# Split weight sums parked in HBM by the first pass and loaded by the second, and one more second-level product group, in a float32 FNet + GEGLU kernel

## The chip, the cores and the metric

One core of a Trainium2 chip runs the whole kernel. The metric is the device time of one execution in microseconds (us), as the median of several runs; less is better.

## The reference

The kernel computes, for x of 2048 rows and 512 columns,

```python
xn = layernorm(x)
a, b = xn @ dft_hid_re.T, xn @ dft_hid_im.T          # 512 x 512 matrices
y = dft_seq_re @ a - dft_seq_im @ b                  # 2048 x 2048 matrices
h = gelu_tanh(xn @ w_gate) * (xn @ w_up)             # 512 x 1792 each
out = x + y + h @ w_down                             # 1792 x 512
```

all in float32.

## The kernel before

Every float32 operand is split into a high and a low part, and each product of two tiles is three matmuls (high-high, low-high, high-low; `mm3`, L332). All large products go through one level of Winograd's form of Strassen's scheme: 2x2 blocks, seven products instead of eight. The products have the numbers 0 to 6 in the code. The operands that the scheme needs are sums of blocks, made on the vector engine (DVE), and split by the scalar engine (ACT, high part) and DVE (low part).

The program has a first half (layer norm, both DFTs; it fills about the first 380 us) and a second half in which the gate and up products are worked off in 28 *units* n = 0 to 27. There are 14 weight blocks (NP = 14) and two passes over them: units 0 to 13 use the first half of the rows of x, units 14 to 27 the second half, with the same weights. A product of a unit is two groups of three matmuls (six). Of the weights a unit loads two tiles `wx` (`load_w`), makes sums `ws` (`weight_sums`, L664), and splits tiles into `wh`/`wl` or, for halves, `w` (`weight_split`). In between stand the down products `dn` and what is left of the DFT (`y`).

For some of the products a second level is used (`inner`). Units n and n+1 (n even) and both passes together form a 2x2 of blocks for product r; seven *inner* products of three matmuls give what four plain products of six would give. `LEAD` says from which unit on this is done: product 0 and 4 from unit 0, product 1 from unit 4. The part of the result that belongs to the second pass is written to HBM (`m_park`, from POOL's queue) and read back by unit n + 14 (`load_m`, SP's queue, tiles `m0`), which then leaves that product out. Where products 0 and 4 are both taken over, the results enter the unit's accumulation in PSUM as a *seed* (an ACT copy).

In the second pass, units 24 to 27 read sums that the first pass had parked (`ws_park`); units 14 to 23 load the weights and make their sums again.

The order of the instructions on each engine is not that of the code: a planner (`Plan`) lists operations with costs, due times, buffer needs (109 slots of 256 KB, `SLOTS`) and limits on transfers in flight, and writes each engine's list from them. A buffer is given to a new tile as soon as the operations that use the old one are over, so an engine can have to wait for a DMA that still reads a buffer which it wants to write, and SP's queue for one that still reads the buffer that it wants to load into. Each engine works its own list in order. `add(name, engine, cost, fn, after, makes, uses, mb)` enters an operation; "p", "v", "a", "g", "s" are TensorE (PE), DVE, ACT, POOL (whose queue writes to HBM) and SP (whose queue reads from it).

Of the kernel before, what the change touches and what calls it, by code (L numbers as in the profile page):

```python
# [39 lines left out]
class Plan:  # L40
# [101 lines left out]
    def choose(self, ready, frees, spare):  # L142
        best = None
        for e, names in ready.items():
# [3 lines left out]
            for n, at in names.items():  # L148
# [134 lines left out]
def fnet_geglu_kernel(ctx: ExitStack, tc: tile.TileContext, x, xt, cs, dh, wgu, wd, out):  # L283
# [81 lines left out]
    m_park = dram.tile([3, NP, P, CH], F32, name="m_park")  # L365
    h_park = dram.tile([NP // 2, 4, P, CH], F32, name="h_park")
    x_park = dram.tile([2, 2, P, CH], F32, name="x_park")
    ws_park = dram.tile([2, NP, 2, P, D], F32, name="ws_park")
# [280 lines left out]
    wx, wl = {}, {}  # L649
# [23 lines left out]
    def trimmed(n, k):  # L673
        return isinstance(n, int) and k < 2 and lead(n - 1, 4 * k)

    def weight_split(n, k):
# [10 lines left out]
        for r, p in enumerate(((0, 1), (4, 5), (6, 2))[k]):  # L687
            wl[n, p] = v[0][:, r], v[1][:, r]
        if trimmed(n, k):
            v, src = ([t.rearrange("p a b -> p (a b)")[:, P:] for t in u] for u in (v, (wx[n][k],)))  # L690
# [10 lines left out]
    LEAD = {0: 0, 4: 0, 1: 4}  # L701
    M_PARK = {0: 0, 4: 1, 1: 2}
    KEEP_SUMS = (10, NP)
# [671 lines left out]
    def unit_at(n):  # L1375
        return TU + n * 17 * 3 * MM + min(max(n, 0), 4) * 2 * W
# [76 lines left out]
    def units():  # L1453

        def weights(m):
            name, at = m if isinstance(m, tuple) else (0, m)
            bare = fetched(m, 1)
            if short(m) or (bare and at >= NP + KEEP_SUMS[0]):
# [21 lines left out]
            for k in range(bool(bare), 3 if short(m) else 4):  # L1480
# [3 lines left out]
                         less=trimmed(m, k))  # L1484
        def park_sums(m, at, d):
# [98 lines left out]
        for r in LEAD:  # L1584
            for n in range(LEAD[r], NP, 2):
# [6 lines left out]
                for j in range(2):  # L1592
                    m = n + NP + j
                    add(("lm", m, r), "s", .45, lambda m=m, r=r: load_m(m, r), after=[("mp", m - NP, r)], mb=MB, makes={("m0", m, r): 1})
# [30 lines left out]
        def inner_p(n, r, k):  # L1625
# [10 lines left out]
            wait = {1: [("sb", n)] if r == 1 else [("ib", n, r)], 5: [("ib", n, r)], 6: [("iq", n, r)], 3: [("iw", n, r)], 2: [("iaw", n, r)]}  # L1636
# [15 lines left out]
        def park_m(n, m, r, to, ready):  # L1652
            add(("mp", m, r), "g", .6, lambda: nc.gpsimd.dma_start(m_park[M_PARK[r], m], side[n, to, r]), after=[ready], uses=[(to, n, r)], mb=MB)

        def plus_first(name, n, m, to):
            u = (n, to, 1)
            add((name, m), "v", V5, lambda: nc.vector.tensor_add(side[u], side[n, to, 0], side[u]),
                after=[("ia" + to[0], n, 1), ("ia" + to[0], n, 0)], uses=[(to, n, 1), (to, n, 0)])
# [320 lines left out]
```

## Time and profile before

| | |
|---|---|
| median of 3 runs | 782.89 us (782.74 to 783.1) |
| the profiled execution | 783.33 us, of which the span of the trace is 781.6 us |
| matmuls | 3432 |
| PE busy | 777.5 us, 99% of the span |
| DVE, ACT, POOL busy | 742.2 us (95%), 531.4 us (68%), 149.5 us (19%) |
| HBM | 131.33 MB read, 69.48 MB written, 257 GB/s over the span |
| granted TensorE clock | full in all 40 slices |

PE, DVE, ACT, POOL and SP are the engines; matmuls overlap, so that one lasts 389 ns in the records while the next starts sooner. "Idle before" in a group's row is the time that its engine stood still ahead of these instructions, and who ended it. A DMA has a time from its issue until its data has landed.

### The profile page before, as it was taken

Reading aid. Unit: us, or ns where it says so; the run is one execution under the profiler, and the core shown is the slowest. Engines: PE = TensorE matmul, PEld = TensorE weight load, DVE = VectorE, ACT = ScalarE, POOL = GpSimd, SP = SyncE. Lnnn points to the kernel's source line nnn. Section 1 sums busy time; section 2 is a strip of 40 time slices with the busy share of each in tenths; the row PEclk is TensorE's granted clock in tenths of the full one; section 3 lists DMA queues with packets and bytes.
Section 4 is the critical chain, followed back from the end, with each engine's and each line's share of the span. In section 5 each row is a group of like instructions: output and inputs, shape, how many; then the busy total and the mean of one; then the engine's idle time right before and its main releaser. Section 6 shows DMA issues by size and latency. Waiting matters only on the chain.

```text
span 781.6 us, 11754 instructions
## 1 busy us (share of the span) xinstructions
PE 777.5 (99%) x3432; PEld 642.2 (82%) x3432; DVE 742.2 (95%) x1410; ACT 531.4 (68%) x1006; POOL 149.5 (19%) x248
## 2 busy tenths in 40 slices
PE   9999999999999999999999999999999999999998
PEld 6888888888888888888888888888888888888887
DVE  7999999999899999999999998999999999997987
ACT  6998565566545374665776766867788887788841
POOL 0120420043221141000212221433100113220000
PEclk9999999999999999999999999999999999999999
DMA  9975997879999979993745544787996468996432
GB/s 329 386 200 164 382 339 245 272 259 274 348 385 387 338 280 377 392 326 118 176 151 160 187 144 156 282 288 273 382 394 238 104 144 161 258 266 215 147 123 108
DMA packets 100465, 198.48 MB, mean 254 GB/s; under 512 B 12176, under 2 KB 20912, under 8 KB 100208
## 3 DMA queue, kind: packets, MB, share of 16 engines
q1 hardware_dynamic: 77616, 134.01, 49.5%
q0 software_dynamic: 22496, 63.45, 27.3%
q8 instruction: 27, 0.44, 0.2%
q14 instruction: 38, 0.31, 0.1%
q10 hardware_dynamic: 288, 0.26, 0.1%
HBM read 131.33 MB, written 69.48 MB: 257 GB/s over the span
## 4 chain that ended last, share of the span: by engine, by line
PE 99%; DMA 0%; DVE 0%; ACT 0%; issue 0%
PE m L332 35%; PE b L332 22%; PE dn L332 17%; PE y L332 10%; PE c L332 8%; PE z L332 4%; PE a L332 3%; DMA x<-in_x 0%; DVE bn L400 0%; DVE p L1915 0%; DVE xa L423 0%; ACT w L411 0%; DVE stats L402 0%; PE st L1266 0%
## 5 line engine op out<-in xcount | busy, mean ns | idle before, releaser
L316 ACT ACTIVATE psh<-pan 128x512 fp32r<-128x512 f32 x203 | 118.2, 627 | 68.4 <-DVE pan L609 27.5
L321 DVE TENSOR_TENSOR psl<-pan,psh 128x512 fp32r<-128x512 f32 x198 | 128.6, 681 | 0.0
L332 PE MATMUL m<-psh,xch 128*128 128x512 f32 x232 | 90.2, 389 | 0.0
L332 PE MATMUL m<-psl,xch 128*128 128x512 f32 x232 | 90.2, 389 | 0.0
L332 PE MATMUL m<-psh,xcl 128*128 128x512 f32 x232 | 90.2, 389 | 0.0
L332 PEld LDWEIGHTS m<-psl,xch 128*128 128x128 f32 x232 | 43.6, 188 | 9.1
L332 PEld LDWEIGHTS m<-psh,xch 128*128 128x128 f32 x232 | 43.6, 188 | 9.1
L332 PEld LDWEIGHTS m<-psh,xcl 128*128 128x128 f32 x232 | 43.5, 188 | 8.9
L1645 ACT ACTIVATE w<-b 128x512 f32<-128x512 f32 x47 | 28.1, 598 | 29.8 <-PE b L332 28.9
L1736 POOL DMA_DIRECT2D partial<-part x28 | 24.5, 896 | 110.5 <-ACT part L1731 99.5
L609 DVE TENSOR_TENSOR pan<-pan 128x512 f32<-128x512 f32 x58 | 38.9, 680 | 3.2 <-DMA pan<-in_cs 3.2
L332 PE MATMUL m<-psh,xa 128*128 128x512 f32 x116 | 40.4, 389 | 0.0
L316 ACT ACTIVATE hth<-s 128x512 fp32r<-128x512 f32 x56 | 33.3, 627 | 10.4 <-DVE s L787 6.7
L1645 ACT ACTIVATE q<-b 128x512 f32<-128x512 f32 x47 | 28.1, 598 | 16.0 <-PE b L332 14.8
L321 DVE TENSOR_TENSOR wl<-ws,wh 128x512 fp32r<-128x512 f32 (+1 forms) x56 | 36.9, 668 | 1.5 <-ACT wh L316 1.3
L787 DVE TENSOR_TENSOR s<-s 128x512 f32<-128x512 f32 x56 | 36.2, 685 | 0.0
L321 DVE TENSOR_TENSOR htl<-s,hth 128x512 fp32r<-128x512 f32 x56 | 36.0, 686 | 0.1
L574 POOL DMA_DIRECT2D partial<-part x28 | 20.8, 790 | 79.0 <-ACT part L570 74.5
L1080 POOL DMA_DIRECT2D t_park<-pan x29 | 16.6, 573 | 98.6 <-DVE pan L610 91.2
L1649 DVE TENSOR_TENSOR w<-c,w 128x512 f32<-128x512 f32 x40 | 27.3, 689 | 6.8 <-ACT w L1645 6.5
L316 ACT ACTIVATE wh<-ws 128x512 fp32r<-128x512 f32 (+1 forms) x56 | 33.2, 609 | 0.0
L332 PE MATMUL dn<-hh,wh 128*128 128x512 f32 x84 | 32.7, 389 | 0.0
(790 smaller groups left out, 2431.9 us busy)
## 6 DMA issues: line engine op xcount, KB each, us to landing
pan<-in_cs SPq DMA_DIRECT2D x157, 256.0 KB, 6.4
partial<-part POOLq DMA_DIRECT2D x56, 256.0 KB, 6.4
wx<-in_wgu SPq DMA_DIRECT2D x48, 256.0 KB, 4.3
m<-m_park SPq DMA_DIRECT2D x38, 256.0 KB, 5.3
t_park<-pan POOLq DMA_DIRECT2D x29, 256.0 KB, 5.6
pan<-t_park SPq DMA_DIRECT2D x29, 256.0 KB, 5.9
h_park<-s POOLq DMA_DIRECT2D x28, 256.0 KB, 4.0
s<-h_park SPq DMA_DIRECT2D x28, 256.0 KB, 5.6
```

The costliest lines, as they stand in the source:

```text
L316: nc.scalar.activation(t[0], src, AF.Copy, scale=float(sign))
L321: engine.tensor_sub(t[1], src, hi)
L332: nc.tensor.matmul(ps, a[u][:, sl], b[v], start=first and r == 0, stop=last and r == 2, skip_group_check=resumed)
L574: nc.gpsimd.dma_start(partial[sp, r, j], ypart.pop((r, j)), **({} if r in (0, 5, 6) else {"accum_op": OP.add}))
L609: return [lambda: nc.vector.tensor_sub(t3, b22, b12), lambda: nc.vector.tensor_sub(t1, b12, b11), lambda: (nc.vector.tensor_sub(b22, *((t1 ...
L787: nc.vector.tensor_sub(t, u, v)
L1080: plan.add(("park", i), "g", .6, lambda: nc.gpsimd.dma_start(t2_park[c, k], pan_src[i][5]), after=[("S", i, 2)], mb=MB, uses=[("r", i, b22)])
L1645: nc.scalar.activation((bank if banks else side)[(n, to, *more)], src(), AF.Copy)
L1649: add((name, n, *more), "v", V5, lambda: nc.vector.tensor_add(side[(n, to, *more)], bank_of(n, c) if c == "c" else bank[(n, c, *more)], si ...
L1736: add(("da", *key), "g", .6, lambda: nc.gpsimd.dma_start(partial[sp, r, j], part[0], accum_op=OP.add), after=[("dc", *key), *sent], uses=[ ...
```

## The change

1. `LEAD[1]` goes from 4 to 2: units 2 and 3 (and with them 16 and 17) also form a second-level group for product 1.
2. The weights' split parts that the second pass needs (product 5, products 6 and 2, product 3; of units 2 to 13) are written to HBM from POOL's queue in the first pass (`park_w`, tensor `w_park`, 1 MB a unit, six DMAs), and units 16 to 27 load them ready to use (`load_half`, `load_whole`, four DMAs of 256 KB a unit). These units no longer load `wx`, make sums or split. Parking of sums (`ws_park`) for the gate and up weights is gone.
3. Additions of the inner products move from the first pass to the second: for product 4 the two summands are copied out by ACT and parked apart (`p2`, `r2`, `m_park` has a fourth part), and unit n + 14 adds them when it seeds its bank, on DVE instead of ACT. For product 1 the addition of the part of product 0 (`plus_first`) is gone, and the second pass adds (`iS`).
4. The planner counts a transfer as at least two when it looks whether a queue has room. The orders of DVE, ACT, SP and POOL change from there on in the first half too, in places; PE's stays the same there.

```diff
-                    k, room = self.parts(o), 8 if e == "s" else 7
+                    k, room = max(self.parts(o), 2), 8 if e == "s" else 7
...
-    LEAD = {0: 0, 4: 0, 1: 4}
-    M_PARK = {0: 0, 4: 1, 1: 2}
-    KEEP_SUMS = (10, NP)
+    LEAD = {0: 0, 4: 0, 1: 2}
+    M_PARK = {0: 0, 4: 1, 1: 2, "4": 3}
+    KEEP_SUMS = (NP, NP)
+    KEEP_SPLIT = 2
...
+            if not name and at >= NP + KEEP_SPLIT:
+                for k, (size, load) in enumerate(((1, load_half), (1, load_half), (2, load_whole), (1, load_half))):
+                    if k == 0 and bare:
+                        continue
+                    add(("lo", ("w", m, k)), "s", .45 * size, lambda k=k, load=load: load(m, k), after=[("pk", at - NP, k)],
+                        makes={("wl", m, k): size}, mb=size * MB, ahead=W_AHEAD)
+                return
...
+                if not name and KEEP_SPLIT <= at < NP and (k or not fetched(m + NP, 1)):
+                    add(("pk", m, k), "g", 1.2 if k < 3 else .6, lambda k=k: park_w(m, k), after=[("lo", ("w", m, k))], uses=[("wl", m, k)],
+                        mb=(1 + (k == 2)) * MB)
+
+        def park_w(m, k):
+            p = (1, 5, 6, 3)[k]
+            for h in range(2):
+                if k == 2:
+                    nc.gpsimd.dma_start(w_park[m, 1 + h], whole[m][h].bitcast(F32))
+                else:
+                    nc.gpsimd.dma_start(w_park[m, k // 3 * 3, :, h], wl[m, p][h].bitcast(F32))
+
+        def load_half(m, k):
+            t = slot("w", F32R, (P, 2, HD))
+            wl[m, (1, 5, 6, 3)[k]] = t[:, 0], t[:, 1]
+            nc.sync.dma_start(t.bitcast(F32), w_park[m - NP, (4, 0, 1, 3)[k]])
...
                     copy("iw", n, "w2", lambda: bank[n, "b2", r], [i], holds=[b2], more=(r,))
-                    sums("iaw", n, "w2", "c2", [("iw", n, r), ("i", n, r, 4)], c2, (r,))
-                    if r == 1:
-                        plus_first("iS", n, n + 1, "w2")
-                    park_m(n, n + 1, r, "w2", ("iS", n + 1) if r == 1 else ("iaw", n, r))
+                    if r != 4:
+                        sums("iaw", n, "w2", "c2", [("iw", n, r), ("i", n, r, 4)], c2, (r,))
+                    park_m(n, n + 1, r, "w2", ("iw" if r == 4 else "iaw", n, r))
+                elif k == 4 and r == 4:
+                    copy("ip", n, "p2", lambda: bank[n, "c2", r], [i], holds=[c2], more=(r,))
+                    park_m(n, n + 1, "4", "p2", ("ip", n, r))
+                elif k == 2 and r == 4:
+                    copy("ir", n, "r2", lambda: bank[n, "c2", r], [i], holds=[c2], more=(r,))
+                    park_m(n, n, "4", "r2", ("ir", n, r))
+                    park_m(n, n, r, "q2", ("iq", n, r))
...
-                nc.scalar.activation(bank[n, place], m0[n, r], AF.Copy)
+                if r == 4:
+                    nc.vector.tensor_add(bank[n, place], m0[n, r], m0[n, "4"])
+                else:
+                    nc.scalar.activation(bank[n, place], m0[n, r], AF.Copy)
...
                 if fetched(n, 1):
-                    hidden(n, (0, 0), [("lm", n, 1)], lambda n=n: m0[n, 1], [], [("m0", n, 1)])
+                    add(("iS", n), "v", V5, lambda n=n: nc.vector.tensor_add(m0[n, 1], m0[n, 0], m0[n, 1]), after=[("lm", n, 0), ("lm", n, 1)],
+                        uses=[("m0", n, 0), ("m0", n, 1)])
+                    hidden(n, (0, 0), [("iS", n)], lambda n=n: m0[n, 1], [], [("m0", n, 1)])
```

In the built programs the counts change as follows: PE 3432 matmuls before, 3429 now; DVE 59 instructions fewer, ACT 35 fewer, POOL 80 DMAs more, SP 36 DMAs more.

PE, product 1 of unit 2 (`a`, weights `wh_4765`/`wl`), in the program before; operands xT10 and xT11 are the two row blocks of the first pass:

```order
L332 MATMUL a_4823<-xT10h_4123,wh_4765 128x512
L332 MATMUL a_4823<-xT10l_4124,wh_4765 128x512
L332 MATMUL a_4823<-xT10h_4123,wl_4766 128x512
L332 MATMUL a_4823<-xT11h_4131,wh_4765 128x512
L332 MATMUL a_4823<-xT11l_4132,wh_4765 128x512
L332 MATMUL a_4823<-xT11h_4131,wl_4766 128x512
```

and in the changed program, the inner products 0 and 1 of the new group of units 2 and 3:

```order
L332 MATMUL b2_5094<-xT10h_4135,wh_4818 128x512 [waits Activation_49]
L332 MATMUL b2_5094<-xT10l_4136,wh_4818 128x512
L332 MATMUL b2_5094<-xT10h_4135,wl_4819 128x512
L332 MATMUL a_4911<-xT11h_4200,wh_4818 128x512
L332 MATMUL a_4911<-xT11l_4201,wh_4818 128x512
L332 MATMUL a_4911<-xT11h_4200,wl_4819 128x512
```

The six matmuls of unit 2 are still there, in two halves with banks of their own; five more inner products of three stand in place of 18 plain matmuls of units 3, 16 and 17.

POOL's queue near the end of the first pass (units 12 and 13), before; `h_park` writes hidden values, `w2`/`q2` are results of inner products, and the semaphores after "waits" are those of an earlier transfer of this queue (DMASW) and of the engine that made the data:

```order
L1653 DMA m_park_81<-w2_6257 128x512 [waits DMASW7_49,DVE_49]
L1653 DMA m_park_81<-q2_6223 128x512 [waits DMASW0_49,DVE_49]
L1753 DMA h_park_82<-s_6101 128x512 [waits DMASW1_49,DVE_49]
L1753 DMA h_park_82<-s_6163 128x512 [waits DMASW2_49,DVE_49]
L1753 DMA h_park_82<-s_6190 128x512 [waits DMASW3_49,DVE_49]
L1653 DMA m_park_81<-w2_6392 128x512 [waits DMASW4_49,DVE_49]
L1653 DMA m_park_81<-q2_6358 128x512 [waits DMASW5_49,DVE_49]
```

and now:

```order
L1692 DMA m_park_81<-r2_6363 128x512 [waits DMASW1_49,Activation_49]
L1795 DMA h_park_82<-s_6266 128x512 [waits DMASW2_49,DVE_49]
L1692 DMA m_park_81<-w2_6389 128x512 [waits DMASW3_49,DVE_49]
L1795 DMA h_park_82<-s_6261 128x512 [waits DMASW4_49,DVE_49]
L1506 DMA w_park_84<-wh_6397 128x512 [waits DMASW5_49,Activation_49]
L1506 DMA w_park_84<-wl_6398 128x512 [waits DMASW6_49,DVE_49]
L1692 DMA m_park_81<-q2_6354 128x512 [waits DMASW7_49,DVE_49]
```

The two `w_park` writes have come in ahead of `q2_6354`. That tile's buffer goes to ACT's copy `w_6533`, which stands among these rows of ACT in the changed program (it waits for DMASW7, the write of `q2_6354`):

```order
L316 ACTIVATE wh_6518<-ws_6365 128x512
L1684 ACTIVATE p2_6524<-c2_6494 128x512 [waits DVE_49,PE_49]
L1684 ACTIVATE w_6533<-b_6444 128x512 [waits DMASW7_49,PE_49]
L1684 ACTIVATE w2_6544<-b2_6419 128x512 [waits PE_49]
L1684 ACTIVATE q2_6553<-b2_6427 128x512 [waits DVE_49,PE_49]
```

PE's matmuls that go on in bank `b_6444` wait for that copy; they start 34 matmuls after the last one that goes into `q2_6354`. Of all chains in the changed program from a matmul over one write to HBM to a matmul it is the shortest; before, the shortest had 49.

SP's queue where the loads for the first units of the second pass stand (16 to 18), before; DMASW3 is the write of the last inner result `q2_6539`:

```order
L655 DMA wx_6681<-in_wgu 128x512 [waits DMAHW1_49,DMASW6_49,DMASW2_49]
L655 DMA wx_6682<-in_wgu 128x512 [waits DMAHW2_49,PE_49]
L1598 DMA m0_6698<-m_park_81 128x512 [waits DMAHW3_49,DVE_49]
L1598 DMA m0_6716<-m_park_81 128x512 [waits DMAHW4_49,DMASW3_49,PE_49]
L655 DMA wx_6741<-in_wgu 128x512 [waits DMAHW5_49,PE_49]
L655 DMA wx_6742<-in_wgu 128x512 [waits DMAHW6_49,PE_49]
```

and now; DMASW4 in the row of `m0_6836` is the write of the last inner result `q2_6688`, whose buffer `m0_6836` gets:

```order
L1637 DMA m0_6836<-m_park_81 128x512 [waits DMAHW0_49,DMASW4_49,PE_49]
L1637 DMA m0_6838<-m_park_81 128x512 [waits DMAHW1_49,DVE_49]
L1513 DMA w_6848<-w_park_84 128x512 [waits DMAHW2_49,Activation_49]
L1520 DMA wh_6851<-w_park_84 128x512 [waits DMAHW3_49,PE_49]
L1520 DMA wl_6852<-w_park_84 128x512 [waits DMAHW4_49,PE_49]
L1513 DMA w_6873<-w_park_84 128x512 [waits DMAHW5_49,DVE_49]
```

Behind the load that waits there are now split weights that PE itself reads (`w_6848` is product 3 of unit 16, its first matmul 73 matmuls after the last one that goes into `q2_6688`), where before there were raw weights.

More of the change, by code (lines that the diff above doesn't have):

```diff
@@ L364, in fnet_geglu_kernel @@
     z_park = dram.tile([NC // 2, 2, 2, 2, P, CH], F32, name="z_park")
-    m_park = dram.tile([3, NP, P, CH], F32, name="m_park")
+    m_park = dram.tile([4, NP, P, CH], F32, name="m_park")
     h_park = dram.tile([NP // 2, 4, P, CH], F32, name="h_park")
     x_park = dram.tile([2, 2, P, CH], F32, name="x_park")
+    w_park = dram.tile([NP, 5, P, 2, HD], F32, name="w_park")
     ws_park = dram.tile([2, NP, 2, P, D], F32, name="ws_park")
@@ L647, in park_xT @@
             nc.gpsimd.dma_start(xT_hl[k, i, h], xT[1, k, i][h].bitcast(F32))
-    wx, wl = {}, {}
+    wx, wl, whole = {}, {}, {}
     def load_w(n):
@@ L673, in trimmed @@
     def trimmed(n, k):
-        return isinstance(n, int) and k < 2 and lead(n - 1, 4 * k)
+        return isinstance(n, int) and k < 2 and lead(n - 1, 4 * k) and 1 + (k == 0 and lead(n - 1, 1))
     def weight_split(n, k):
@@ L688, in weight_split @@
             wl[n, p] = v[0][:, r], v[1][:, r]
+        whole[n] = v
         if trimmed(n, k):
-            v, src = ([t.rearrange("p a b -> p (a b)")[:, P:] for t in u] for u in (v, (wx[n][k],)))
+            if k == 0 and lead(n - 1, 1):
+                v, src = ([t[:, :, P:] for t in u] for u in (v, (wx[n][k],)))
+            else:
+                v, src = ([t.rearrange("p a b -> p (a b)")[:, P:] for t in u] for u in (v, (wx[n][k],)))
             return v, src[0]
@@ L1375, in unit_at @@
     def unit_at(n):
-        return TU + n * 17 * 3 * MM + min(max(n, 0), 4) * 2 * W
+        return TU + n * 17 * 3 * MM + min(max(n, 0), 2) * 4 * W
     for k in range(HS):
@@ L1484, in weights, with load_whole @@
                          less=trimmed(m, k))
+                if not name and KEEP_SPLIT <= at < NP and (k or not fetched(m + NP, 1)):
[12 more added lines that the diff above has]
+            nc.sync.dma_start(t.bitcast(F32), w_park[m - NP, (4, 0, 1, 3)[k]])
+        def load_whole(m, k):
+            v = slot("wh", F32R, (P, 2, HD)), slot("wl", F32R, (P, 2, HD))
+            for r, p in enumerate((6, 2)):
+                wl[m, p] = v[0][:, r], v[1][:, r]
+            for h in range(2):
+                nc.sync.dma_start(v[h].bitcast(F32), w_park[m - NP, 1 + h])
         def park_sums(m, at, d):
@@ L1593, in units @@
                     m = n + NP + j
+                    if r == 4:
+                        add(("lm", m, "4"), "s", .45, lambda m=m: load_m(m, "4"), after=[("mp", m - NP, "4")], mb=MB, makes={("m0", m, "4"): 1})
                     add(("lm", m, r), "s", .45, lambda m=m, r=r: load_m(m, r), after=[("mp", m - NP, r)], mb=MB, makes={("m0", m, r): 1})
@@ L1652, in park_m @@
         def park_m(n, m, r, to, ready):
[L1653 to L1658, printed above, removed]
+            add(("mp", m, r), "g", .6, lambda: nc.gpsimd.dma_start(m_park[M_PARK[r], m], side[n, to, int(r)]), after=[ready], uses=[(to, n, int(r))], mb=MB)
         def first_block(n, m, to, ready, held):
@@ L1699, in f @@
                 bank[n, place] = ps_tile(place)
-                nc.scalar.activation(bank[n, place], m0[n, r], AF.Copy)
-            add((name, n), "a", A5, f, after=[("p", n - 1, 5 if place == "b" and fetched(n, 1) else 6), ("lm", n, r)], banks=[key], holds=[key], uses=[("m0", n, r)])
-        until = 4
+                if r == 4:
+                    nc.vector.tensor_add(bank[n, place], m0[n, r], m0[n, "4"])
+                else:
+                    nc.scalar.activation(bank[n, place], m0[n, r], AF.Copy)
+            both = [r, "4"][:1 + (r == 4)]
+            add((name, n), "v" if r == 4 else "a", V5 if r == 4 else A5, f, after=[("p", n - 1, 5 if place == "b" and fetched(n, 1) else 6), *(("lm", n, u) for u in both)], banks=[key], holds=[key], uses=[("m0", n, u) for u in both])
+        until = 2
         todo = [("y", r, j, g) for r in (5, 3) for j in range(2) for g in range(2)]
```

6 lines of the change are left out of this document (2 added, 4 removed).

## The prediction

> **What bounds the kernel now.** I read the page's busy line and its chain first, then the list of PE's waits, then the chain in order of time, and last the second half in stretches.
>
> ```profile
> PE 777.5 (99%) x3432; PEld 642.2 (82%) x3432; DVE 742.2 (95%) x1410; ACT 531.4 (68%) x1006; POOL 149.5 (19%) x248
> PE 99%; DMA 0%; DVE 0%; ACT 0%; issue 0%
> ```
>
> PE is busy 99% of the span and is the whole chain that ends last. DVE is close behind at 95%, so the two have to be told apart by who waits for whom. The list of PE's waits has one row:
>
> ```profile
> PE warm L828 <- PEq L1972: 0.8, 1, 0.8
> ```
>
> That is 0.8 us, once, at the very start. After it no matmul waited for DVE, ACT or a DMA long enough to be listed. The chain in order of time says the same; its columns are start, length, engine and tile:
>
> ```profile
> 5.44 33.49 PE z L332 x144
> ...
> 97.56 76.16 PE m L332 x336
> ```
>
> ```profile
> 759.88 18.52 PE dn L332 x93
> 778.40 0.02 issue
> 778.43 0.42 DVE p L1915
> ```
>
> Here 336 matmuls take 76.16 us, which is 0.2267 us each, and PE goes on from 5.44 to 778.40 us without a piece of anything else. So PE's time is its number of matmuls times 0.2267 us, with some 8.6 us at both ends (5.44 us until the first real matmul, 3.2 us after the last), and nothing else has a price as long as PE does not have to wait. DVE's 95% is cover that is used up nearly, but not beyond.
>
> One rule speaks against reading it so. The Trainium skill, in "Perfetto Trace Analysis", section "Identifying the Most-Contended Engine", says that matmul busy time is a poor measure and that the share of weight loads is to be used; by that PE stands at 82% and DVE at 95% would be the most contended engine. The trace decides by the missing waits; what the rule would make of the time is the last rival below.
>
> **The matmuls.** The new group takes product 1 of units 2, 3, 16 and 17: four plain products of six matmuls, 24, become seven inner ones of three, 21. That is the only change in PE's count, 3432 to 3429: 3 x 0.2267 = 0.68 us less. It lies on the path from end to end, since PE is the path.
>
> **DVE and ACT.** What leaves DVE are mainly sums and low splits of weights in the second pass; what comes are 26 additions of parked summands there. The rows that price them (line, operands, count, busy, mean ns):
>
> ```profile
> L664 DVE TENSOR_TENSOR ws<-wx 128x256 f32<-128x256 f32 x45 | 18.8, 418 | 0.0
> L321 DVE TENSOR_TENSOR wl<-ws,wh 128x512 fp32r<-128x512 f32 (+1 forms) x55 | 36.2, 668 | 1.5 <-ACT wh L316 1.3
> L774 DVE TENSOR_TENSOR s<-s,m 128x512 f32<-128x512 f32 x5 | 3.4, 685 | 0.2 <-ACT s L769 0.2
> L1649 DVE TENSOR_TENSOR q<-c,q 128x512 f32<-128x512 f32 x40 | 27.4, 684 | 0.5 <-PE c L332 0.3
> ```
>
> ```profile
> L1645 ACT ACTIVATE w<-b 128x512 f32<-128x512 f32 x47 | 28.1, 598 | 29.8 <-PE b L332 28.9
> ```
>
> ```profile
> L332 PE MATMUL m<-psh,xch 128*128 128x512 f32 x232 | 90.2, 389 | 0.0
> ```
>
> 58 instructions of 256 columns x 0.418 = 24.2 us, 12 low splits x 0.668 = 8.0 us and 22 additions of the first pass x 0.685 = 15.1 us go, 47.3 us; 26 additions x 0.685 = 17.8 us and seven instructions for the new group, about 3 us, come. Net about 26 us off DVE (742 to 716 us), and 35 activations at up to 0.60 us, 21 us at most, off ACT, although ACT gets 14 more copies in the first pass. On PE's path all this is worth nothing: no wait of PE on DVE or ACT is there to be removed. It costs nothing either. PE's shortest round through ACT has 6 matmuls in between in both programs (7 x 0.2267 = 1.59 us, against 0.39 us of a matmul and 0.60 us of a copy), and DVE only gets more room.
>
> **The transfers.** This is where the change can cost something. POOL issues 80 DMAs more, nearly all in the first pass; SP 36 more, in the second. In bytes that is about 15 MB more to write and 10 MB more to read on 198 MB. What matters is how long data take to land. The stretches of the end of the first pass and the start of the second (PE, PEld, DVE, ACT, POOL busy; clock, DMA share, GB/s):
>
> ```profile
> 535.00:550.00 15.00, 15.00 (x68) 12.43 (x67) 14.32 (x29) 11.31 (x21) 4.24 (x8) 1.00 0.86 309
> 550.00:565.00 15.00, 15.00 (x67) 12.41 (x67) 14.22 (x31) 10.62 (x22) 2.91 (x6) 1.00 1.03 382
> 565.00:580.00 15.00, 15.00 (x68) 12.42 (x67) 14.02 (x30) 11.29 (x24) 1.98 (x4) 1.00 1.05 400
> 595.00:610.00 15.00, 15.00 (x68) 12.43 (x67) 14.49 (x34) 13.71 (x28) 0.00 (x0) 1.00 0.23 82
> ```
>
> The DMA engines are full from 550 us on (the slices up to 595 us are alike) and mostly idle from 595 us, so before they ran ahead of the need there; the clock is full and PE never stops. The landing times of the parked inner results, written by POOL (530 to 560 us), and of all transfers of that tensor (560 to 600 us):
>
> ```profile
> L1653 POOL DMA_DIRECT2D m_park<-q x4: 542/542/542, 534.9 to 559.9; - x4
> ...
> DMA to landing us min/median/max: 3.6/5.5/6.7
> ```
>
> ```profile
> L1598 SPq DMA_DIRECT2D m<-m_park x13: 319/327/411, 561.8 to 595.4; - x13
> ...
> DMA to landing us min/median/max: 4.5/5.5/8.3
> ```
>
> *First place*, unit 13, near 541 us (counted back from the end, 1054 matmuls of which 24 are half ones): a write of an inner result holds the buffer that ACT's copy needs, and PE needs the copy 34 matmuls after the one that made the result. Time there: 34 x 0.2267 = 7.7 us. It takes 0.39 (matmul) + 0.68 (DVE sum) + 0.60 (copy) = 1.7 us beside the write, so 6.0 us are left for issue and landing. An issue keeps POOL for 0.54 us, so that 80 more take 43 us of an engine that is busy 19% of the span; that alone holds up nothing. The landing row, counted from the issue, says 3.6 to 6.7 us: from 2.4 us to spare to 0.7 us late. Two `w_park` writes now go just ahead of it. I take the median, 5.5 us, and no wait, 0.7 us as the upper end.
>
> *Second place*, unit 16, near 566 us: SP's queue stands at the load of `m0_6836` until the write of the last inner result is through, and the split weights behind it are read by PE directly. From the last matmul of that result to the first that reads `w_6848` there are 73 matmuls, 16.5 us. Needed: 0.39 + 0.68, the write's landing, the issues of the two loads ahead, 2 x 0.33 = 0.7 us, and the load's own landing. At the medians 1.1 + 5.5 + 0.7 + 5.5 = 12.8 us, 3.7 us to spare; at the maxima 1.1 + 6.7 + 0.7 + 8.3 = 16.8 us, 0.3 us late. The same load feeds DVE, which is in order, and a sum behind it is needed by PE 79 matmuls later, 17.9 us: with 4 x 0.685 = 2.7 us for DVE's instructions 1.1 + 5.5 + 5.5 + 2.7 = 14.8 us at the medians, 18.8 us at the maxima, 0.9 us late (the late ends overlap, so 0.9 us holds for both). Such standing of SP's queue is nothing new (waits of SP's queue: total, times, longest):
>
> ```profile
> SPq L1598 <- DMA m_park<-w: 27.0, 5, 8.1
> SPq L1598 <- DMA m_park<-q: 13.3, 4, 6.3
> ```
>
> It stood up to 8.1 us and PE did not notice. The loads behind have more room: the fifth (`w_6873`) is read 91 matmuls after, 20.6 us.
>
> A rule bears on this stretch. The Trainium skill, "HBM Reference", "Specifications (TRN2)", gives about 358 GB/s as a core's share, and about 425 GB/s for a core that streams alone. The row of 400 GB/s fits the second. By the first, an estimate, loads would land 400/358 = 12% later, 6.2 us instead of 5.5 us, which the second place still bears.
>
> So the middle of both unknown costs is 0 us, and their upper ends add up to 0.7 + 0.9 = 1.6 us. Below nothing they cannot go: there is no listed wait to win back.
>
> **The first half** is reordered a little on DVE, ACT, SP and POOL (where single transfers now count as two), with PE's order unchanged. PE had no wait there, and the same dependences stay, so I cost it at nothing; what covers it is again PE's queue of work.
>
> **The sum.** 783.33 - 0.68 = 782.65 us against the profiled execution. That one was 0.44 us above the median of the runs (782.89 us), so against the median 782.89 - 0.68 = 782.21 us. With 1.6 us of waits it would be 783.8 us.
>
> **Rivals.** *The forecast*, fewer matmuls and at most 1.6 us of new waits: 782.2 us (to 783.8), a change of -0.09% to +0.12%. I take 0.2%, 1.57 us, as what a measurement of this kernel can tell from no change, so this whole case counts as the same. Chance 0.80.
>
> *Slower: both queues full at the hand-over.* With 8 transfers of SP and 7 of POOL in flight, 15 x 0.262 MB at 400 GB/s take 9.8 us. If the additional writes fill POOL's queue up to the end of the first pass, both hops of the second place take that long: 1.1 + 9.8 + 0.7 + 9.8 = 21.4 us against 16.5 us, 4.9 us late, and the time is 782.2 + 4.9 = 787.1 us. It decides from 2.25 us of waiting (1.57 + 0.68), which is when the two landings together pass 17.0 us. For it speaks that the DMA engines are full there already; against it that the largest landing seen is 8.3 us with SP's queue full, that POOL is over with its writes soon after, and the idle 595 to 610 us. Chance 0.16.
>
> *Faster: DVE was the bound in truth.* Then the 26 us that it loses would show, 782.9 - 26 = 757 us. Its 95% speak for it, the one row of PE's waits against. Chance 0.02. (The section of "Perfetto Trace Analysis" in the Trainium skill that is named above would have it so.) The same again, 0.02, for some gain of over 1.57 us at the start or the end, of which the rows show none.
>
> *The change does not do what it says*, that is PE's count is down by three but the group's own round trips cost those 0.68 us again: 782.9 us. It lies in the first case.
>
> **How the numbers follow.** 782.2 us is the time of the likeliest case. Of its 0.80 I put the low end at 781.9 us (the runs spread 0.36 us) and the high end at 784.0 us, 783.8 us with half that spread; what is left out is the slower case but for its mildest part, and the faster one. Faster 0.04, same 0.80, slower 0.16.
>
> **What would show it.** In the changed profile: 3429 matmuls at 0.2267 us, PE still 99% of the chain, DVE near 716 us, ACT near 510 to 515 us, POOL near 193 us, some 223 MB moved, and no row among PE's waits but the first. A wait of `b` on ACT `w` near 541 us would be the first place; a wait of `b` on a DMA `w<-w_park` or of `c` on DVE `w` near 569 us the second. The prediction is wrong if such rows add up to over 2.25 us, or if PE's first matmul or the tail after the last has moved.

## The result, and the profile after

The changed kernel takes 787.17 us (785.27 to 789.24, 6 runs); the kernel before took 782.83 us beside it. The ratio is 1.0059, with a 95% interval of 1.0041 to 1.0076: 4.3 us or 0.6% slower. The forecast was 782.2 us and no change that can be measured. The profiled execution took 787.01 us, its span is 785.2 us, 3.6 us more than before.

Busy times, what was moved and the chain that ended last, from the page of the changed kernel:

```profile
PE 778.4 (99%) x3429; PEld 641.2 (82%) x3429; DVE 720.6 (92%) x1351; ACT 518.3 (66%) x971; POOL 192.1 (24%) x328
DMA packets 110515, 223.66 MB, mean 285 GB/s; under 512 B 14033, under 2 KB 21745, under 8 KB 110257
PE 96%; DMA 2%; ACT 1%; DVE 1%; issue 0%; DVEq 0%; ACTq 0%
```

The counts are those forecast or near them: 3429 matmuls, DVE 720.6 us where 716 was forecast, ACT 518.3 us where it was 510 to 515, 223.66 MB where it was 223. But the chain is no longer PE alone: PE is 96% of it, and not 99%. The list of PE's waits (total, times, longest) has two rows that it did not have:

```profile
PE b L332 <- ACT q L1684: 2.3, 2, 1.6
PE warm L834 <- PEq L2016: 0.8, 1, 0.8
PE m L332 <- ACT m L1116: 0.2, 1, 0.2
```

The list shows only what is idle time; measured as the time from one matmul to the next beyond 0.2267 us, the stops after the first 9 us add up to 4.06 us, against 0.09 us before: 0.85 us near 333 to 335 us (first half), 1.02 us at 509 us, 0.18 us at 512 us and 1.85 us at 561.7 us. With the 0.09 us of before and the three matmuls taken off, 4.06 - 0.09 - 0.68 = 3.3 us of the 3.6 us are accounted for; most of the rest is the tail after the last matmul, 3.4 us instead of 3.2 us.

The chain in order of time (start, length, engine and line) shows how the longest stop came about:

```profile
548.51 1.12 PE b L332 x5
549.63 9.21 DMA m<-m_park
558.84 0.03 issue
...
558.97 0.70 DVE m L1862
...
559.69 0.04 ACT s L775
...
560.23 0.58 ACT p L1684
560.81 0.30 ACT w L316
561.11 0.50 ACT q L1684
561.61 0.04 issue
561.65 2.34 PE b L332 x9
```

A load of a parked inner result takes 9.21 us to land. DVE stands at L1862, the addition `iS` that was moved into the second pass, until it is there. Behind it ACT stands at L775, the gelu of the sum, and behind that, in ACT's queue, the copies `p` and `q` and a split `w`. PE needs `q` and stops. The same chain stands before 509 us, with a load of 7.16 us. Neither of the two places named in the prediction (541 us and 566 us) has a stop.

### The profile page after: what moved, and what is told of

Read it like the earlier page. It is cut to its first block, busy times and chain, and to the rows that moved or that the text cites. A ratio compares the mean times of both kernels' runs of the same rounds, so it can differ in the third digit from the quotient of the medians.

```text
span 785.2 us, 11961 instructions
## 1 busy us (share of the span) xinstructions
PE 778.4 (99%) x3429; PEld 641.2 (82%) x3429; DVE 720.6 (92%) x1351; ACT 518.3 (66%) x971; POOL 192.1 (24%) x328
## 2 busy tenths in 40 slices
DMA packets 110515, 223.66 MB, mean 285 GB/s; under 512 B 14033, under 2 KB 21745, under 8 KB 110257
## 4 chain that ended last, share of the span: by engine, by line
PE 96%; DMA 2%; ACT 1%; DVE 1%; issue 0%; DVEq 0%; ACTq 0%
PE m L332 35%; PE b L332 20%; PE dn L332 17%; PE y L332 10%; PE c L332 8%; PE z L332 4%; DMA m<-m_park 2%; PE a L332 2%; PE warm L834 1%; DVE m L1862 0%; ACT wh L316 0%; ACT q L1684 0%; DVE c L1119 0%; DVE wil L321 0%; ACT wih L316 0%
## 5 line engine op out<-in xcount | busy, mean ns | idle before, releaser
L321 DVE TENSOR_TENSOR psl<-pan,psh 128x512 fp32r<-128x512 f32 x198 | 128.3, 680 | 0.0
L332 PE MATMUL m<-psh,xch 128*128 128x512 f32 x232 | 90.4, 389 | 0.1
L332 PE MATMUL m<-psl,xch 128*128 128x512 f32 x232 | 90.3, 389 | 0.0
L332 PE MATMUL m<-psh,xcl 128*128 128x512 f32 x232 | 90.3, 389 | 0.0
L332 PEld LDWEIGHTS m<-psh,xch 128*128 128x128 f32 x232 | 43.5, 188 | 9.6 <-DVE m L1121 0.5
L332 PEld LDWEIGHTS m<-psh,xcl 128*128 128x128 f32 x232 | 43.6, 188 | 9.1
L332 PEld LDWEIGHTS m<-psl,xch 128*128 128x128 f32 x232 | 43.6, 188 | 8.9
L332 PE MATMUL m<-psh,xa 128*128 128x512 f32 x116 | 40.4, 389 | 0.0
L321 DVE TENSOR_TENSOR htl<-s,hth 128x512 fp32r<-128x512 f32 x56 | 35.8, 682 | 1.4 <-ACT hth L316 1.3
L321 DVE TENSOR_TENSOR hl<-s,hh 128x512 fp32r<-128x512 f32 x42 | 27.2, 684 | 8.0 <-ACT hh L316 7.9
L332 PE MATMUL dn<-hh,wh 128*128 128x512 f32 x84 | 32.7, 389 | 0.0
L332 PE MATMUL dn<-hh,wl 128*128 128x512 f32 x84 | 32.7, 389 | 0.0
L332 PE MATMUL dn<-hl,wh 128*128 128x512 f32 x84 | 32.7, 389 | 0.0
```

The lines of the kernel that those rows point to most:

```text
L321: engine.tensor_sub(t[1], src, hi)
L332: nc.tensor.matmul(ps, a[u][:, sl], b[v], start=first and r == 0, stop=last and r == 2, skip_group_check=resumed)
```

## The experiments

Four explanations were held against each other. *Queue*: the moved addition stands first in DVE's queue, and what is behind it is late. *Traffic*: the writes of split weights make transfers land later, whoever waits for them. *Order*: each new order of the planner meets stops of some size somewhere. And for the first half, the planner's line that counts a transfer as two. Each kernel was timed beside the kernel before, 782.76 to 782.81 us in all of these comparisons.

### Parts undone, with the planner ordering anew

Product 1's addition back in the first pass:

```diff
+                    if r == 1:
+                        plus_first("iS", n, n + 1, "w2")
...
-                    add(("iS", n), "v", V5, lambda n=n: nc.vector.tensor_add(m0[n, 1], m0[n, 0], m0[n, 1]), ...
-                    hidden(n, (0, 0), [("iS", n)], lambda n=n: m0[n, 1], [], [("m0", n, 1)])
+                    hidden(n, (0, 0), [("lm", n, 1)], lambda n=n: m0[n, 1], [], [("m0", n, 1)])
```

> The changed kernel, but the addition of product 0's part to product 1's part stands in the first pass again, and the second pass's gelu reads the parked sum as before. Queue theory (the moved addition stands first in DVE's queue until two loads have landed, ACT's gelu stands behind it, ACT's copies behind that, and PE behind the copies): the waits of PE in the second half, 3.1 us in the trace of the changed kernel, go or fall below 0.7 us; the 0.9 us in the first half near 333 us stays; 784 us (783.5 to 784.8). Traffic theory (the writes and loads of split weights make every landing longer, whoever waits for it): ACT's gelu waits for its load itself and PE waits as long; 786.5 to 787.5 us. Order theory (any new order of the planner meets waits of that size by chance): waits somewhere else, 784 to 788 us.

Measured: 783.50 us, ratio 1.0008 (1.0000 to 1.0017). No stop is left in the second half; 0.9 us near 333 us stay.

No split weights parked:

```diff
-    KEEP_SUMS = (NP, NP)
-    KEEP_SPLIT = 2
+    KEEP_SUMS = (10, NP)
+    KEEP_SPLIT = NP
```

> The changed kernel without the parking of split weights: no split weights are written or loaded, units 14 to 23 of the second pass load and split weights and units 24 to 27 read parked sums, as in the kernel before. The moved additions and the additional group stay. Traffic theory: landings of the parked inner results fall back to the 5.5 us median of before, no wait of PE in the second half, 783.1 us with the 0.9 us of the first half left (782.2 without). Queue theory: the addition still waits for two loads at the head of DVE's queue, so at least 1.5 of the 3.1 us stay: 784 to 787 us. Order theory: anything from 783 to 787 us, with waits at other places.

Measured: 786.58 us, 1.0048 (1.0036 to 1.0061). 1.3 us remain at 559 us, behind the moved addition, and 2.05 us are new near 612 to 621 us, where the units split weights again and DVE is at 95% of the span: `PE dn L332 <- DVE wl L321: 1.1, 2, 0.6` among PE's waits. The load behind the stop at 559 us took 7.14 us to land although no split weights were written; from 500 to 560 us this order moved 317 GB/s. Taken by themselves these two runs speak for *queue* and against *traffic*. They would have been the story, had the planner's order been the same; it was not, and the next runs show that this matters.

The planner's line alone, in the kernel before, and undone, in the changed kernel:

```diff
-                    k, room = self.parts(o), 8 if e == "s" else 7
+                    k, room = max(self.parts(o), 2), 8 if e == "s" else 7
```

> The kernel before with one line of the change alone: the planner counts a transfer as at least two. The same matmuls, additions and transfers in another order. By the reading of the trace this line makes the wait near 333 us of the first half: 0.9 us, 783.7 us, a wait of m on ACT m among PE's waits and none in the second half. By the prediction, which costed the first half at nothing: 782.8 us. Order theory: waits in the second half too, 784 us or more.

```diff
-                    k, room = max(self.parts(o), 2), 8 if e == "s" else 7
+                    k, room = max(self.parts(o), 2 * (n[0] == 'pk')), 8 if e == "s" else 7
```

> The changed kernel with that line undone, except that a write of split weights (two DMAs) still counts as two: the first half has the order of before. By the reading of the trace the 0.9 us near 333 us go and the second half keeps waits behind the moved addition: about 786.3 us. If the line's effect on the second half is what made those waits: below 784 us. Order theory: anything from 783 to 788 us.

Measured: 783.86 us for the line alone, 1.0013 (1.0004 to 1.0022), that is 1.0 us (0.3 to 1.7 us); PE's waits name the first half (0.98 us of stops near 333 us, and 0.37 us at 477 us):

```profile
PE m L332 <- ACT m L1110: 0.3, 1, 0.3
```

So the planner's line, costed at nothing, costs about 1 us; most of its stops lie in the first half, and the one at 477 us, which was not expected, in the second. The line undone in the changed kernel gives 797.86 us, 1.0190 (1.0176 to 1.0204), far outside of what any reading of mine expected:

```profile
PE b L332 <- ACT wh L316: 6.4, 1, 6.4
PE b L332 <- ACT q L1684: 2.7, 1, 2.7
PE c L332 <- DVE w L1688: 1.2, 1, 1.2
```

2.7 us is the moved addition again, at 562 us. The 6.4 us at 618 us are put down to an ACT split that was long done; the load of `wh` from `w_park` that PE reads there was issued at 612.7 us and landed at 618.0 us. SP's queue had stood 3.9 us and 2.9 us between 572 and 579 us for writes to `m_park`, and from 595 us on it issued a load about every 0.65 us, each one after an earlier load had landed; the DMA engines were full there (share 1.05 and 386 GB/s from 595 to 612 us). This is what the prediction feared for its second place (split weights that PE reads directly, behind a late queue), in another order and 50 us later.

### The parts alone

The group alone, in the kernel before, with its order of the first half:

```diff
-    LEAD = {0: 0, 4: 0, 1: 4}
+    LEAD = {0: 0, 4: 0, 1: 2}
...
-        return TU + n * 17 * 3 * MM + min(max(n, 0), 4) * 2 * W
+        return TU + n * 17 * 3 * MM + min(max(n, 0), 2) * 4 * W
...
-        until = 4
+        until = 2
```

> The kernel before with the additional second-level group alone (units 2, 3, 16, 17): no split weights parked, additions in the first pass, planner as before. Three matmuls less, 0.68 us: 782.1 us (781.9 to 782.5) if the group has no wait of its own. If the group's round trips cost its gain: 782.8 us. If DVE's load (95% of the span, and the group adds to it) has no room for the group: above 783 us, with a wait of PE on DVE.

Measured: 786.34 us, 1.0046 (1.0034 to 1.0058). Three matmuls less, and 3.5 us slower. No transfer stands in the chains up to its stops; PE's waits, and the chain up to one of them:

```profile
PE c L332 <- DVE s L774: 2.2, 2, 1.2
...
PE c L332 <- DVE q L1649: 0.6, 1, 0.6
```

```profile
515.94 0.68 DVE wil L321
516.62 0.20 DVE wi L741
516.82 0.60 DVE q L1649
517.42 0.64 DVE e L1662
...
519.78 0.68 DVE wil L321
520.47 0.61 DVE s L774
521.08 0.04 issue
521.12 0.96 PE c L332 x3
```

DVE works without a pause from 515.3 us on and comes to the instruction that PE needs 1.2 us late. In this order the group needs room on DVE that the first pass does not have. Is it the moved additions of product 4 that make it? They were put back in the changed kernel, and moved alone beside the group:

```diff
-                    if r != 4:
-                        sums("iaw", n, "w2", "c2", [("iw", n, r), ("i", n, r, 4)], c2, (r,))
+                    sums("iaw", n, "w2", "c2", [("iw", n, r), ("i", n, r, 4)], c2, (r,))
...
```

> The changed kernel, but the additions of product 4 stand in the first pass again (14 on DVE instead of copies on ACT, 0.685 us each, 9.6 us; 14 writes fewer), and the second pass seeds from one parked tile on ACT. If the group needs that room on DVE: waits of c on DVE s or DVE q in the first pass as in the group alone (near 443, 508, 521 us), 786 to 789 us. If not: the 14 writes fewer make 786.5 us or less, with no wait on DVE in the first pass.

> The group and the moved additions of product 4 alone: no split weights parked, product 1's addition in the first pass, the first half in the order of before (a transfer counts as two only in the second half). If moved additions of product 4 are the room that the group lacked: no wait in the first pass, 782.1 us (782.0 to 782.6), faster than before by the three matmuls. If the second pass, with its splits and sums and 14 additions more on DVE, has no room: waits of PE on DVE w or wl after 600 us, 783.5 us or more.

Measured: 789.34 us with them back, 1.0089 (1.0075 to 1.0103), with PE waiting for DVE in the first pass (`c` on DVE `s` 0.6 us at 521 us, on DVE `w` 2.1 us at 558 us). That is not only a want of room on DVE: ahead of the wait at 558 us DVE itself stood 1.7 us for a write to `m_park` that took 6.77 us, and in two more stops, at 505 and 533 us, PE waits 2.9 us for ACT (`PE b L332 <- ACT s L775: 2.9, 2, 1.7`). It is 785.67 us for the group with them moved, 1.0034 (1.0021 to 1.0046), with no stop in the first pass, and one of 2.0 us at 612 us in the second, where ACT works from 605 to 612 us without a pause (`PE dn L332 <- ACT s L775: 1.9, 1, 1.9`). That the moved additions of product 4 make the room thus rests on the last run, in which the stops of the group alone are gone; as the planner ordered anew, it is likely and not shown. The price turned up in the second pass, where the weights of that run are still split.

### The order held

In the runs above the planner wrote new orders, so that each compares two things at once. The following five leave all that the planner sees as it is and change what an operation does: the rows of PE, DVE, ACT and SP keep their order.

No wait at the moved additions (additions out, the gelus and products read another tile), and the additions alone left out:

```diff
-                    add(("iS", n), "v", V5, lambda n=n: nc.vector.tensor_add(m0[n, 1], m0[n, 0], m0[n, 1]), ...
-                    hidden(n, (0, 0), [("iS", n)], lambda n=n: m0[n, 1], [], [("m0", n, 1)])
+                    add(("iS", n), "v", V5, lambda: None, ...
+                    hidden(n, (0, 0), [("iS", n)], lambda n=n: xT[1, 1, n % 2][0].bitcast(F32), [], [("m0", n, 1)])
```

> The changed kernel with every engine's order as it is, but in units 16 to 27 the twelve moved additions of product 1 are left out and the instructions behind them (ACT's gelus, DVE's products) read a tile that has lain in the buffer since the first pass instead of the loaded sum. Nothing in DVE's or ACT's queue waits for these loads any more; all transfers remain. Queue theory: the 3.1 us of waits in the second half are gone, the first half's 0.9 to 1.1 us stay: 783.3 us (782.9 to 783.8). Traffic theory or a general shortage of ACT or DVE: the waits stay, 786 us or more.

> As the kernel before this one, but only the additions are left out: the gelus and products read the loaded tile of product 1, which ACT and DVE wait for themselves. If ACT's standing at the head of its queue until the load has landed is what PE feels: 785.5 to 787.5 us, waits of PE near 509 and 561 us as in the changed kernel. If DVE's standing at the addition is needed for it: 783.3 us.

Measured: 787.19 us with the additions out and another tile read, 1.0055 (1.0042 to 1.0068). The queue theory said 783.3 us, and falls here. The stop at 509 us is gone and the one at 562 us is down to 0.77 us, but two are new (551 us 1.39 us, 554 us 0.64 us). What DVE waited for, from 380 to 620 us:

```profile
DVE s L780 <- DMA m_park<-w: 3.7, 2, 2.9
DVE xT31l L321 <- DMA h_park<-s: 2.7, 1, 2.7
DVE c L1739 <- DMA m<-m_park: 1.7, 1, 1.7
```

Where DVE does not stand at the addition, it stands at the next thing that a late transfer holds: writes to `m_park` and `h_park` that still read a buffer, and a load. The stop at 551 us does not even need DVE: there ACT stands 1.7 us for a write to `m_park` before its copy `w`, on which PE waits. The stop at 562 us is a less clean case, because the tile that is read instead had just been loaded anew there (8.41 us to land), and ACT's gelu stood 2.0 us for it. With the addition alone left out it is 786.01 us, 1.0042 (1.0030 to 1.0054), with ACT standing at the gelu itself (`ACT s L775 <- DMA m<-m_park: 5.3, 2, 3.2`, 450 to 600 us) and the stops at 509 us and 562 us as before: DVE's part in it is not needed.

Split weights written for one unit alone; and all the writes there, but small:

```diff
-            for h in range(2):
+            for h in range(2 * (m == KEEP_SPLIT)):
...
-            nc.sync.dma_start(t.bitcast(F32), w_park[m - NP, (4, 0, 1, 3)[k]])
+            nc.sync.dma_start(t.bitcast(F32), w_park[KEEP_SPLIT, (4, 0, 1, 3)[k]])
```

> The changed kernel, every engine's order kept, but split weights are written for unit 2 alone, and units 16 to 27 all load those: 55 DMAs fewer on POOL's queue, 14 MB less to write, the same loads. Traffic theory, now with the order held: the loads of parked results land in 5.5 us instead of 7 to 9 us, the waits behind them shrink by 1.5 to 3 us each, 783.5 us. If the landings owe nothing to those writes: 786.5 to 787.5 us.

```diff
+            rows = P if m == KEEP_SPLIT else 8
...
-                    nc.gpsimd.dma_start(w_park[m, 1 + h], whole[m][h].bitcast(F32))
+                    nc.gpsimd.dma_start(w_park[m, 1 + h, :rows], whole[m][h][:rows].bitcast(F32))
```

> The changed kernel, every engine's order kept and every DMA there, but from unit 3 on a write of split weights takes 8 of the 128 partitions (a sixteenth of its bytes), and units 16 to 27 all load unit 2's. If the bytes on the DMA engines make the waits: as without the writes, 783.3 us (782.9 to 783.8). If it is the 55 more entries in POOL's queue that hold up the writes behind them: the waits stay, 786 to 787.5 us. In between, a share of each.

Measured: 783.30 us without those writes, 1.0010 (1.0001 to 1.0019), and 783.63 us with small ones, 1.0012 (1.0003 to 1.0021). In both the second half has no stop at all; what is left is the first half's 0.8 us. So with the order held the writes of split weights carry the whole loss of the second half, and they do it by their bytes (11.55 MB less are moved without them), not by their 66 entries in POOL's queue (the expectations had counted 14 MB and 55 entries). The stretch from 500 to 560 us (PE, PEld, DVE, ACT, POOL busy; clock, DMA share, GB/s), in the changed kernel, without the writes and with small ones:

```profile
500.00:560.00 60.00, 59.25 (x260) 48.24 (x258) 51.68 (x112) 42.61 (x82) 32.71 (x61) 1.00 0.96 349
```

```profile
500.00:560.00 60.00, 60.00 (x267) 49.67 (x266) 55.14 (x119) 46.31 (x90) 17.82 (x33) 1.00 0.84 294
```

```profile
500.00:560.00 60.00, 60.00 (x267) 49.67 (x266) 54.54 (x118) 46.41 (x90) 31.47 (x60) 1.00 0.88 299
```

POOL's count is nearly the same in the first and the third, the rate is not: 349 against 299 GB/s. And the two loads that the stop at 561.7 us hangs on, in the changed kernel and without the writes:

```profile
L1637 SPq DMA_DIRECT2D m<-m_park x2: 412/493/574, 549.0 to 549.6; - x2
...
  DVE m L1862: 2.7, 1
...
DMA to landing us min/median/max: 8.1/8.7/9.2
```

```profile
L1637 SPq DMA_DIRECT2D m<-m_park x2: 371/376/382, 546.8 to 547.3; - x2
...
DMA to landing us min/median/max: 6.1/6.2/6.3
```

That is 2.5 us of landing at the median, and the stop was 1.85 us; with small writes the two loads took 6.4 and 6.5 us.

### The order made to wait less

The planner took parked results to land 2.5 us later, first with nothing else changed, then with the first half in the order of before; and the first again with its order held and the writes left out.

```diff
-            self.ends[n] = end
+            self.ends[n] = end + 2.5 * (n[0] == 'lm')
```

> The changed kernel with one number more in the planner: a load of a parked inner result is taken to land 2.5 us later than planned. All instructions, PE's order and nearly all of SP's stay; in the queues of DVE and ACT the moved additions and the gelus behind them come later, behind other work. Queue theory (the wait costs because of what stands behind it): the 3.1 us in the second half go although the loads land no sooner; the 0.9 to 1.1 us of the first half stay; 783.5 us (783.2 to 784.3), as with the addition back in the first pass. If what matters is that the second pass adds at all, or that the loads land late: 786 to 787 us.

> The whole change, with the order of before in the first half (a transfer counts as two only in the second) and the parked results taken to land 2.5 us later. Nothing of the change is undone but the planner's line in the first half. Queue theory: 782.1 us (782.0 to 782.7). If moved additions or split parking have a cost of their own: 783.5 us or more.

> The kernel in which parked results are taken to land 2.5 us later (790.0 us; DVE stood 5.8 us at a sum of weights whose buffer a write of split weights still read, and PE 3.6 us behind it), with its order kept and split weights written for unit 2 alone. If that write is the cause: PE's wait of 3.6 us goes, 785.5 to 786.5 us or less. If DVE's wait is for something else that only looked like the write: no change, 789 to 791 us.

Measured: 790.02 us (1.0093, 1.0080 to 1.0106), 788.93 us (1.0080, 1.0068 to 1.0092), and 784.33 us without the writes (1.0020, 1.0011 to 1.0029). The stops at the addition were gone, and DVE stood at a sum of weights instead. The chain of the first of the three:

```profile
557.82 5.34 DMA w_park<-w
563.15 0.09 DVE ws L665
...
565.52 0.61 DVE w L1688
566.13 0.04 issue
566.17 0.96 PE b L332 x3
```

A write of split weights still reads the buffer that the sum goes into. Without the writes PE's wait of 3.6 us there is gone, as that theory wanted; a stop of 1.0 us at 585 us is left, with two of the moved additions in its chain. In the second of the three the sum stood behind a load of weights that took 10.28 us, and PE 3.2 us behind it.

### Which part can be kept

Product 1's addition in the first pass, the first half in the order of before, and split weights parked for 12, 8 and 6 units; and the whole change with 6 (`halfway` is 340 us; the cut shows `KEEP_SPLIT` for 8 units, which is 2 for 12 units and 8 for 6):

```diff
-                    k, room = max(self.parts(o), 2), 8 if e == "s" else 7
+                    k, room = max(self.parts(o), 2 * (self.clock["p"] > self.halfway)), 8 if e == "s" else 7
...
-    KEEP_SPLIT = 2
+    KEEP_SPLIT = 6
```

> The kernel with product 1's addition back in the first pass, and besides the planner counts a transfer as two only in the second half, so that the first half has the order of before. If the two causes (the addition's wait and the new order of the first half) are all that the change cost: the three matmuls are left, 782.81 - 0.68 = 782.1 us (782.0 to 782.6), no wait of PE but the first. Order theory: a new order of the second half has waits of its own, 783 to 786 us.

> As the kernel that parks six units' split weights with product 1's additions in the first pass and the first half as before, but for units 6 to 13, eight of twelve. If bytes of the first pass and DVE's room in the second are the two sides: between the neighbours, 782.3 to 783.3 us, and a gain on before only if both waits (near 533 us behind a late write, 0.7 us, and near 613 us behind ACT, 0.6 us) are gone. If every new order has its own waits: 783 to 786 us at new places.

> As the kernel with product 1's addition in the first pass and the first half as before (783.1 us, 782.1 to 785.5), but split weights are parked for units 8 to 13 only, six instead of twelve: 30 DMAs and 6 to 8 MB less to write. If the split writes still cost there what made its runs differ by 3 us: 782.1 to 782.5 us with a small spread. If units 16 to 21 now lack room on DVE: waits behind DVE between 560 and 600 us, 783 us or more.

> The whole change with the first half as before and split weights parked for units 8 to 13 only. By the bytes: 206 to 214 MB instead of 224 MB and fewer writes before 500 us, so the waits at the moved additions shrink to below 1 us in all: 782.3 to 783.3 us. If the writes of units 8 to 13, which fall between 480 and 560 us, are those that count: 785 to 787 us with a wait near 560 us.

Measured: 783.10 us with 12 units (1.0008, 0.9999 to 1.0016; runs from 782.14 to 785.51 us), 782.83 us with 8 (1.0005, 0.9996 to 1.0013; 782.46 to 784.28 us), 783.48 us with 6 (1.0011, 1.0002 to 1.0020), and 791.46 us for the whole change with 6 (1.0107, 1.0091 to 1.0122). The last is above both of its forecasts: the stop at 562 us behind the moved addition is there, 3.8 us long, with a load of 8.50 us, and more stops follow from 617 us on. Best is the one with 8 units: its profiled execution has 0.21 us of stops and a span of 780.5 us, but over its runs it is level with the kernel before. No version was faster than before.

One pattern runs through the runs in which the planner ordered anew. With product 1's addition in the second pass: 787.2, 786.6, 797.9, 790.0, 788.9, 789.3 and 791.5 us. With it in the first: 783.5, 783.1, 782.8 and 783.5 us where split weights were parked, 785.7 and 786.3 us where not, which is no better than the 786.6 us above without parked split weights. What goes with it in the traces are SP's loads of parked results between 380 and 560 us, in the changed kernel and with the addition back:

```profile
L1637 SPq DMA_DIRECT2D m<-m_park x24: 319/327/987, 432.0 to 557.2; - x24
```

```profile
L1637 SPq DMA_DIRECT2D m<-m_park x14: 319/326/929, 446.2 to 553.1; - x14
```

and the standing of SP's queue until a result that was just written may be loaded (380 to 620 us), again in the changed kernel and with the addition back:

```profile
SPq L1637 <- DMA m_park<-q: 55.8, 8, 16.8
```

```profile
SPq L1637 <- DMA m_park<-q: 4.7, 5, 2.3
```

The addition needs both summands at once, and the planner brings them, ten loads more, into the end of the first pass, where writes fill the DMA engines. That this is why those orders are worse was not isolated: no run held the order and moved only those loads.

## Why the prediction was wrong

- *PE bounds the kernel, at 0.2267 us a matmul, and stops are the only other price.* Right: stops of 4.06 us and 0.68 us less explain 3.3 of the 3.6 us.
- *The transfers*, "upper ends add up to 0.7 + 0.9 = 1.6 us", is the term that failed; it was 3.1 us in the profiled execution. It failed twice. The places were chosen by where PE is reached over one write or directly by a load. The change adds a wait on two loads to DVE, and the prediction did not follow what stands behind it: DVE's queue, ACT's gelu, ACT's copies, PE. That path alone is not the cause, since with the wait at its head left out the time stayed at 787.19 us. And the price of a landing was taken from the rows of before (5.5 us at the median, 8.3 us at most), although the change itself adds the writes: the loads took 8.1 to 9.2 us there, and up to 12.0 us, and with the writes shrunk and the order held the stops were gone.
- *DVE's relief is worth nothing, and the group only gets its matmuls less.* Wrong, as far as the runs go: the group alone cost 3.5 us behind a full DVE, so the relief seems to pay for the group and not to stand beside it; each of these runs has an order of its own. That DVE was no bound in the kernel before, as the sentence on the most contended engine had it, is right only for that kernel's order: with nine instructions more (1419 for 1410; the prediction took seven), PE waited for DVE.
- *The first half costs nothing.* Wrong by about 1 us (0.3 to 1.7 us), shown by the planner's line alone, 0.98 of its 1.35 us of stops being in the first half.
- *The slower rival*, "both queues full at the hand-over", gave 787.1 us, and the time measured is 787.17 us. Its cause was half right: the DMA engines were full and the writes' bytes did it. Its place and its sum were not: SP's queue did stand, up to 16.8 us, but that was from 414 us on, long before the hand-over. At the hand-over the write of the last inner result took 5.83 us and the load of `w` 4.43 us, together 10.3 us and not over the 17.0 us that were its condition, and `w` lay there at 585.0 us, 2.0 us before PE read it. Agreement of the two numbers is chance.

What stays open is how much of the loss belongs to the moved addition's order of loads and how much to luck of the order. The experiments with the order held settle that in this order the bytes decide; across orders the place of the addition went with 3.7 us (787.17 against 783.50 us) and 8.0 us (791.46 against 783.48 us) where split weights were parked, but each new order also had stops of its own. Open is also how the bytes divide between other transfers that land later and buffers that a write of split weights itself holds.

## What to carry to other kernels

A bound engine that never waits does not say how near it is to waiting: read what stands at the head of the other engines' queues, and for each added wait on a DMA follow the queue behind it up to the bound engine. Price a landing in the traffic of the changed kernel, not of the one before: here 11.55 MB more of writes made two loads land in 8.1 and 9.2 us instead of 6.1 and 6.3 us. And where a planner writes the order, undoing a part compares two orders: hold the order and change what an operation does, before a cause is named.

## What the runs showed of the hardware

A stop of PE can cost more than its own length. In the whole change with six units, PE stops for 3.67 us up to 562.3 us, and then runs at half the granted clock for 5.1 us (PE, PEld, DVE, ACT, POOL busy; clock, DMA share, GB/s):

```profile
562.30:567.40 5.10, 5.08 (x12) 4.02 (x13) 3.44 (x9) 2.22 (x5) 0.00 (x0) 0.50 1.05 397
568.00:573.00 5.00, 5.00 (x24) 4.14 (x23) 3.85 (x8) 3.21 (x8) 2.11 (x4) 1.00 1.05 396
```

That is 12 matmuls where 24 go in 5 us at the full clock. A clock of 0.50 followed waits of 6.4, 3.6 and 3.2 us in three other runs too, for 3.3 to 4.1 us of matmuls. After the wait of 3.6 us it came late: PE went on at 1.00 from 566.2 to 567.4 us and stood at 0.50 from 567.5 to 570.8 us. After 2.7 us (at 562 us with the planner's line undone) the clock stayed at 1.00. The Trainium skill, "TensorE: Matmul & The Clock Gate", "Part 1: The HAM clock gate (the "warmup" mystery)", says that about 3.4 us without work put the array back to half its clock until it has been busy for as long; the trace agrees, with 0.50 in the row above; where between 2.7 and 3.2 us of waiting it begins, no run here shows. It would fit the changed kernel's own runs: four of its six, with a mean granted clock of 1.0, took 785.3 to 787.3 us, and two, with 0.998, took 789.1 and 789.2 us, as if there the stop at 562 us had passed that length. Those two have no trace here.
